# Four instead of two W_in blocks of the first pair in one-pass products, in a new instruction order

## The chip, the cores and the metric

The kernel runs on one core of one Trainium2 chip. The metric is the device time of one execution, in microseconds (us), as the median of the runs. The names of the engines in the profile are PE (matrix products), PEld (the loading of weights into PE), DVE, ACT, POOL and SP; SP only issues transfers here.

## What is computed

A chunked state-space scan over x, a, B and C (4 batches, 8 heads, 768 steps, head width 32, state width 16) gives 3072 rows of 256 numbers. These rows go through two matrix products with a silu between them.

```python
for c in range(nc):
    ...
    L = np.exp(cum[:, :, :, None] - cum[:, :, None, :]) * causal
    CB = np.einsum('bhin,bhjn->bhij', Cc, Bc)
    y_intra = np.einsum('bhij,bhjd->bhid', CB * L, xc)
    y_inter = np.einsum('bhin,bhnd->bhid', Cc, state) * decay_to_i[:, :, :, None]
    y[:, :, sl] = y_intra + y_inter
    state = decay_full[:, :, None, None] * state + np.sum(Bx, axis=2)
...
h = x @ w_in                          # (3072, 256) @ (256, 2048)
g = h * (1.0 / (1.0 + np.exp(-h)))
return g @ w_out                      # (3072, 2048) @ (2048, 256)
```

## The kernel before

The 3072 rows are worked on in 12 units of 256 rows; two units make a pair, so there are six pairs, 0 to 5. For each unit u the scan is a short chain over four engines: products of B and C (`g0`, line 585), products of x and B (`D` for units 0 and 1, `gd` later, line 571), a decay scan on DVE (`E`, line 512), the masking product on DVE (`M`, line 600, two halves), the running state on DVE (`S`, line 615) and its copy on ACT (`SM`, line 623), and at the end the unit's rows in PSUM (`Y`, lines 635 and 644).

W_in and W_out are each cut into 8 blocks, numbered 0 to 7 (W_in) and 8 to 15 (W_out). They arrive as 64-bit numbers, 512 KB a block (`lw`, line 288), and each is made into a 32-bit block by two ACT instructions (`u`, line 294, and `v`, line 297), three DVE instructions (`w,n,0`, `w,n,1`, `w,n,2`, lines 303, 307, 310) and an addition on POOL (`W`, line 318).

There are two ways to multiply by a block. In 32-bit form PE takes every product in two passes that the trace lists as two records; that is `s,u,j` (line 697: unit u, W_in block j) and `n1` (line 761: W_out for pair 0). In the other way both factors are split into three parts, named h, l and d: a rounded high part, the rest, and a correction. The product of the parts h and l (`a,G,i`, line 800) and of the parts d (`d,G,i`, the same line) goes for a whole pair at once in one pass for each part; `q` (line 782) is the same for W_out, with `qh` for the parts h and l and `qd` for d. `ax` and `dg` (lines 811 and 821, ACT) scale the sum between them and apply silu. The parts of a weight block come from `H` (ACT, line 322), `lD` (DVE, line 326) and `dD` (DVE, line 330), or for some W_out blocks from ACT copies and POOL transfers (`Wl`, `Wd`, `Wm`, `We`); the parts of a unit's rows come from `xh` (ACT, line 679) and `x,u,0` and `x,u,1` (DVE, lines 651 and 654, the l and the d part). For the silu outputs they are `h` (ACT, line 827), `l` (DVE, line 651) and `e` (DVE, line 837).

Pairs 1 to 5 use parts throughout. Pair 0 is done as the weights arrive: six of its eight W_in blocks in 32-bit form (`s`, each unit by itself, silu by `si`, line 703) and blocks 6 and 7 in parts (`a,0,6`, `a,0,7`); its W_out product is in 32-bit form (`n1`). For the 32-bit form a unit's rows are copied out of PSUM to one tile by `X0,u,0` and `X0,u,1` (ACT, line 666); `s` and `xh` read that tile. Products of even blocks are summed in the PSUM tile ga and those of odd blocks in gb, the two tiles that `g0`, `gd` and `Y` use too.

The order is written out by hand as a list of words, `SCHEDULE` (lines 18 to 100). Each word calls the function of that name and so appends its instructions to the in-order queues of the engines that it uses; no scheduler changes the order after that. `SLOTS` names the buffer that each tile takes in turn. The word `z,1` is a product of zeros that PE runs while it waits at the start (line 441). Loads with a queue number 0 go out by SP in the order of the list.

## Time and profile before

| what | us |
|---|---|
| median of three runs (329.33 to 329.74) | 329.33 |
| the profiled execution | 329.1 |
| its span, first to last instruction | 327.4 |
| PE busy in the span | 320.3 |
| DVE busy | 240.4 |
| ACT busy | 209.5 |
| POOL busy | 56.0 |

The profiled execution's own time is 1.7 us longer than its span, and 0.23 us shorter than the median. Times within the span are counted from its start. A matrix product's listed duration is its latency; consecutive products overlap, so what one costs on PE is seen from where a row of them starts and where the next one does. The same holds, to a smaller part, on DVE and ACT, where an instruction starts about 0.08 us before the one ahead of it is listed as ended.

### The profile page before, as it was taken

To read this page: it belongs to the slowest core of one execution; us is meant where nothing else is said; L and a number is where in the kernel's file an instruction comes from. 1 tells how busy PE (TensorE), PEld (TensorE's weight loads), DVE (VectorE), ACT (ScalarE), POOL (GpSimd) and SP (SyncE) were. 2 spreads that over 40 slices of the span, in tenths; PEclk is the share of its full clock that TensorE was granted. 3 is DMA by queue.
4 is the path that set the end of the run, shared out by engine and by line. 5 is a ranking of instruction groups with operands and counts; after the bars stand their busy time and mean duration, and the time that the engine had idled before them with its cause. 6 is when DMAs were issued, how large, how long until landed. Compare 5 with 4: busy or idle time off the path is not lost.

```text
span 327.4 us, 7519 instructions
## 1 busy us (share of the span) xinstructions
PE 320.3 (98%) x3064; PEld 243.4 (74%) x3067; DVE 240.4 (73%) x331; ACT 209.5 (64%) x319; POOL 56.0 (17%) x74
## 2 busy tenths in 40 slices
PE   8999999999999999999999999999999999999994
PEld 3478576655687777878887778878887788888883
DVE  4998999999988965877687299665787544635553
ACT  4679978648696846583771875837775455574641
POOL 1364766326102330001200010010001000000000
PEclk9999999999999999999999999999999999999999
DMA  6979966479872663423633306514042000050003
GB/s 162 206 200 272 296 175 192 51 148 135 148 127 46 105 115 53 86 36 64 147 74 70 44 1 117 104 26 96 3 74 37 7 2 2 0 88 0 2 1 64
DMA packets 94962, 29.27 MB, mean 89 GB/s; under 512 B 80000, under 2 KB 86912, under 8 KB 94928
## 3 DMA queue, kind: packets, MB, share of 16 engines
q1 hardware_dynamic: 90960, 25.71, 37.5%
q0 software_dynamic: 1616, 2.82, 5.1%
q10 hardware_dynamic: 2352, 0.26, 0.6%
q8 instruction: 24, 0.39, 0.5%
q14 instruction: 10, 0.08, 0.1%
HBM read 22.81 MB, written 3.34 MB: 80 GB/s over the span
## 4 chain that ended last, share of the span: by engine, by line
PE 94%; SPq 2%; DMA 1%; DVE 1%; issue 1%; DVEq 0%
PE hp L782 29%; PE ga L800 18%; PE gb L800 18%; PE hp L761 9%; PE hp L697 6%; PE o_ps L782 6%; PE ga L635 2%; PE ga L585 2%; PE ga L644 2%; DMA s2k<-in_C_dram 1%; PE gb L644 1%; PE ga L571 1%; SPq L262 0%; SPq L375 0%; PE o_ps L531 0%
## 5 line engine op out<-in xcount | busy, mean ns | idle before, releaser
L782 PE MATMUL hp<-r4k,s2k 128*128 128x512 f32 x400 | 110.0, 394 | 0.0
L651 DVE SCALAR_TENSOR_TENSOR r4k<-r4k,r4k 128x1024 fp32r<-128x1024 f32 (+1 forms) x42 | 50.5, 1202 | 51.3 <-ACT r4k L827 48.2
L782 PEld LDWEIGHTS hp<-r4k,s2k 128*128 128x128 f32 x400 | 74.0, 188 | 16.4 <-issue 0.3
L800 PE MATMUL ga<-raw,s2k 128*128 128x512 f32 x240 | 62.3, 395 | 0.0
L800 PE MATMUL gb<-raw,s2k 128*128 128x512 f32 x240 | 61.1, 390 | 0.0
L800 PEld LDWEIGHTS ga<-raw,s2k 128*128 128x128 f32 x240 | 44.7, 188 | 11.4 <-ACT ga L811 0.9
L800 PEld LDWEIGHTS gb<-raw,s2k 128*128 128x128 f32 x240 | 44.8, 188 | 9.9 <-ACT gb L811 0.5
L837 DVE SCALAR_TENSOR_TENSOR r4k<-r4k,r4k 128x1024 fp32r<-128x1024 f32 x40 | 49.2, 1231 | 3.4 <-DVE r4k L651 0.9
L827 ACT ACTIVATE r4k<-r4k 128x1024 fp32r<-128x1024 f32 x40 | 42.2, 1058 | 3.2 <-issue 1.3
L811 ACT ACTIVATE ga<-ga 128x1024 f32<-128x1024 f32 x21 | 21.1, 1007 | 24.6 <-PE ga L800 23.8
L811 ACT ACTIVATE gb<-gb 128x1024 f32<-128x1024 f32 x21 | 21.2, 1009 | 17.6 <-PE gb L800 13.3
L782 PE MATMUL o_ps<-r4k,s2k 128*128 128x512 f32 x80 | 30.7, 390 | 0.0
L761 PE MATMUL hp<-r4k,s2k 128*128 128x512 f32 x64 | 30.0, 602 | 0.0
L821 ACT ACTIVATE r4k<-gb 128x1024 f32<-128x1024 f32 x21 | 21.4, 1021 | 12.4 <-PE gb L800 9.9
L520 POOL TENSOR_TENSOR BT<-bn,ab 128x256 f32<-128x256 f32 x10 | 6.7, 672 | 129.5 <-DVE ab L512 123.3
L318 POOL TENSOR_TENSOR s2k<-s2k,s2k 128x512 uint32<-128x512 uint32 (+1 forms) x19 | 23.6, 1250 | 26.4 <-DVE s2k L307 13.7
L821 ACT ACTIVATE r4k<-ga 128x1024 f32<-128x1024 f32 x21 | 21.5, 1023 | 8.4 <-PE ga L800 8.2
L512 DVE TENSOR_TENSOR_SCAN ab<-ab,diag 128x512 f32<-128x512 f32 x20 | 24.8, 1265 | 0.0
L697 PE MATMUL hp<-r4k,s2k 128*128 128x256 f32 x96 | 22.3, 382 | 0.2 <-issue 0.2
L697 PEld LDWEIGHTS hp<-r4k,s2k 128*128 128x128 f32 x96 | 18.0, 190 | 4.0 <-issue 1.4
L761 PEld LDWEIGHTS hp<-r4k,s2k 128*128 128x128 f32 x64 | 11.6, 189 | 10.5 <-issue 9.6
L782 PEld LDWEIGHTS o_ps<-r4k,s2k 128*128 128x128 f32 x80 | 15.0, 188 | 3.2
(123 smaller groups left out, 384.8 us busy)
## 6 DMA issues: line engine op xcount, KB each, us to landing
ab<-az SPq DMA_DIRECT2D x20, 256.0 KB, 4.2
raw<-in_moe_w_in_dram SPq DMA_DIRECT2D x8, 512.0 KB, 4.2
raw<-in_moe_w_out_dram SPq DMA_DIRECT2D x8, 512.0 KB, 8.0
out_dram<-r4k SPq DMA_DIRECT2D x44, 64.0 KB, 2.0
xt<-in_x_dram SPq DMA_DIRECT2D x20, 128.0 KB, 4.2
s2k<-s2k POOLq DMA_DIRECT2D x10, 256.0 KB, 3.8
pfx<-ac SPq DMA_DIRECT2D x10, 130.0 KB
bn<-in_B_dram SPq DMA_DIRECT2D x20, 64.0 KB, 5.2
```

The lines of the kernel that those rows point to most:

```text
L318: nc.gpsimd.tensor_tensor(out=u[:, :, fs], in0=u[:, :, fs], in1=v[:, :, fs], op=ALU.add)
L512: nc.vector.tensor_tensor_scan(out=o, data0=src, data1=diag.rearrange("p h t -> p (h t)"), initial=0.0, op0=ALU.mult, op1=ALU.add)
L644: nc.tensor.matmul(out=y[w][32 * q:32 * q + 32, c, 64 * k:64 * k + 64], lhsT=xc[64 * c:64 * c + 64, k, h], rhs=m[64 * c:64 * c + 64, k, h] ...
L651: nc.vector.scalar_tensor_tensor(out=l, in0=f32(h), scalar=BACK, in1=y, op0=ALU.mult, op1=ALU.add)
L697: nc.tensor.matmul(out=hp[:, i], lhsT=WT[j][:, kc, 128 * i:128 * i + 128], rhs=XM()[:, 2 * kc:2 * kc + 2, u], start=(kc == 0), stop=(kc == ...
L761: nc.tensor.matmul(out=NP[m], lhsT=WT[8 + f // 2][:, f % 2, 128 * m:128 * m + 128], rhs=GT[0, f // 2][:, f % 2], start=(n == 1), stop=(n = ...
L782: nc.tensor.matmul(out=ACC[P, c], lhsT=WK[8 + i, p][:, k, 128 * m:128 * m + 128], rhs={"h": HT, "l": LT, "d": DT}[p][P, i][:, k], start=(n ...
L800: nc.tensor.matmul(out=o, lhsT=WK[j, q][:, kc, 128 * i:128 * i + 128], rhs=xs[:, 2 * kc:2 * kc + 2], start=(start and q == "h" and kc == 0 ...
L811: nc.scalar.activation(t, t, AF.Copy, scale=1.0 + Z)
L821: nc.scalar.activation(g, t, AF.Silu, scale=BACK)
L827: nc.scalar.activation(t, GT[G, i], AF.Copy, scale=-LESS * Z)
L837: nc.vector.scalar_tensor_tensor(out=DT[G, i], in0=f32(HT[G, i]), scalar=-1.0, in1=f32(LT[G, i]), op0=ALU.mult, op1=ALU.subtract)
```

## The change

Blocks 4 and 5 of W_in move, for pair 0, from the 32-bit form to parts. The words `s,0,4`, `s,1,4`, `s,0,5`, `s,1,5` and their four `si` go; `a,0,4`, `a,0,5`, `ax`, `d` and `dg` for the same two blocks come. No other word is added or removed: the other 1301 words are those of before, in another order, and so are the buffers that the tiles take. W_in blocks are loaded in the order 0, 5, 4, 2, 6, 1, 7, 3 instead of 0, 4, 7, 5, 1, 6, 2, 3. The first blocks that PE multiplies are 0 and 2 in 32-bit form and then 5 and 6 in parts; before they were 0, 4, 5 for unit 0, then 1, 5, 0, 4 and then 7 in parts. One of the 36 products of zeros ahead of the transpose `AT` moves behind it. All functions below line 102 are unchanged but for the buffer numbers in `SLOTS`.

The diff of the list at the start, at the first pair, around the start of pair 1's W_out products, and at the end:

```diff
 SCHEDULE = """
-Ln,0,0,0,1 ia,1 ci z,1 z,1 z,1 z,1 z,1 z,1 ia,0 Ln,0,0,1,1 cI z,1 ch cP ct ip,0,0 z,1 z,1 z,1 c1 cd A AT cp AU lw,0 z,1
+ci ch z,1 Ln,0,0,0,1 ia,1 z,1 Ln,0,0,1,1 ia,0 z,1 z,1 z,1 c1 cd cp cI co z,1 z,1 ip,0,0 A cP ct z,1 z,1 lw,0 AT AU
+as,1,1 as,0,0 tp,0 tq,0 P01,0,0 ab,0,0 z,1 z,1 z,1 z,1 Lx,0,0,0 as,0,1 P01,0,1 ab,0,1 Lt,0,1,3,0 E,0,0 B,0,0 u,0 w,0,0
 ...
-S,0,3 Ln,1,1,0,0 ab,1,0 E,1,0 C,0 Y,0 X0,0,1 Ln,1,0,1,0 B,1,1 X0,0,0 u,5 w,5,0 ip,1,0 z,1 P01,1,0 tp,1 tq,1 s,0,0 ce,1,1
-ce,1,0 g0,1 Lx,1,1,0 Lx,1,0,0 W,4 xh,0 w,5,1 si,0,0 B,1,0 P01,1,1 D,1 s,0,4 M,1,1 lw,1 u,1 lw,12 S,1,0 W,5 v,1 ca S,1,1
-S,1,2 SM,1,0 SM,1,1 lw,13 s,0,5 si,0,5 v,12 C,1 M,1,0 Y,1 w,1,0 w,1,1 W,7 si,0,4 lw,8 w,1,2 W,1,0 z,1 w,12,2 X0,1,0 H,7
-S,1,3 X0,1,1 x,0,0 lD,7 u,12 w,12,0 w,12,1 u,13 w,13,0 w,13,1 W,1,1 s,0,1 u,8 v,8 s,1,5 ir,3 w,8,0 si,0,1 s,1,0 co
-Ln,2,0,1,0 xh,1 W,12 x,1,0 w,8,1 v,13 w,13,2 W,13 lw,15 u,15 w,8,2 Ln,2,1,1,0 si,1,5 s,1,4 a,0,7 si,1,4 n1,9,0 H,12
-Wd,12 x,0,1 lw,14 u,14 n1,11,0 n1,9,1 x,1,1 W,8 Ln,2,1,0,0 v,14 w,14,2 ir,0 si,1,0 n1,1,0 n1,1,1 H,0 n1,0,1 H,1 lw,6 v,6
+z,1 z,1 z,1 M,0,1 ab,1,0 z,1 w,5,1 SM,0,1 lw,2 z,1 v,4 w,4,2 u,4 w,4,0 z,1 W,0,0 z,1 H,0 Ln,1,0,0,0 SM,0,0 C,0 z,1 w,5,2
+W,5 v,2 Y,0 w,4,1 u,2 Ln,1,0,1,0 E,1,0 Ln,1,1,0,0 X0,0,0 X0,0,1 xh,0 H,5 tp,1 tq,1 ce,1,0 w,2,2 ce,1,1 s,0,0 ip,1,0
+S,0,3 w,2,0 P01,1,0 w,2,1 P01,1,1 C,1 B,1,0 si,0,0 ca B,1,1 Lx,1,0,0 Lx,1,1,0 D,1 S,1,0 g0,1 S,1,1 S,1,2 SM,1,0 W,2,1
+W,2,0 s,0,2 M,1,0 W,4 lw,6 Ln,2,0,1,0 M,1,1 SM,1,1 Y,1 lD,5 v,6 w,6,2 u,6 w,6,0 X0,1,1 lw,1 x,0,0 X0,1,0 H,4 z,1 w,6,1
+x,0,1 s,1,0 W,6 ir,0 lw,10 lw,7 xh,1 S,1,3 u,1 w,1,0 H,6 x,1,1 x,1,0 w,1,1 v,1 w,1,2 W,1,1 Ln,2,1,1,0 s,1,2 u,10 lD,6
+lw,8 si,1,2 v,10 w,10,0 a,0,5 si,1,0 a,0,6 ax,0,6 w,10,1 si,0,2 ir,2 ir,1 w,10,2 u,7 W,1,0 s,0,1 u,8 W,10 v,8 ir,3 v,7
+s,1,1 dD,5 Ln,2,0,0,0 si,0,1 lw,3 v,3 n1,5,1 Ln,2,1,0,0 AA,0 Lt,3,1,0,0 dD,6 d,0,6 w,8,0 AD,4 H,10 Wl,10 n1,5,0 u,3
+dg,0,6 ax,0,5 w,8,2 w,7,0 n1,4,0 lD,4 tp,2 w,7,2 n1,4,1 lw,13 u,13 w,7,1 W,7 ce,2,0 H,7 w,8,1 W,8 w,3,0 a,0,4 n1,1,1
 ...
-u,2 W,6 n1,8,0 AD,1 v,2 H,6 v,10 w,2,0 s,1,1 si,1,1 lw,3 tp,2 dD,7 v,3 v,15 u,3 w,2,1 w,2,2 W,2,0 Lt,3,1,3,0 lD,6 dD,6
-w,14,0 n1,8,1 w,3,2 a,0,6 ax,0,6 w,15,2 W,2,1 s,1,2 si,1,2 H,2 d,0,7 w,14,1 dg,0,7 AD,2 w,3,0 w,15,1 d,0,6 dg,0,6 W,14
-Lt,3,1,0,0 w,10,2 s,0,2 lw,9 u,9 v,9 Lt,3,1,2,0 Lt,3,1,1,0 T,3,1 H,4 si,0,2 n1,10,0 Lx,2,0,0 n1,12,1 La,2,0,0 w,3,1 tq,2
-La,2,1,0 E,2,1 E,2,0 lD,4 w,9,0 W,15 n1,15,1 Lt,3,0,0,0 n1,12,0 B,2 ce,2,0 ce,2,1 Lt,3,0,3,0 g0,2 lw,11 u,11 Lp,2,0 C,2
-M,2,1 Lx,2,1,0 gd,2 b,2,0 b,2,1 S,2,0 S,2,1 H,15 S,2,2 W,3 Lp,3,0 Lt,4,1,1,0 H,13 La,3,1,0 w,10,0 v,11 Lt,4,1,0,0
-n1,15,0 SM,2,0 Wl,15 SM,2,1 w,10,1 W,10 ce,3,1 Lt,4,1,3,0 M,2,0 La,3,0,0 E,3,1 E,3,0 s,0,3 si,0,3 Lt,3,0,2,0 ce,3,0
+n1,0,1 w,3,1 AA,1 d,0,5 lw,15 v,15 w,13,0 AP AD,0 v,13 si,1,1 ce,2,1 dg,0,5 lw,14 w,13,1 lD,7 w,13,2 W,13 n1,0,0 w,3,2
+W,3 n1,1,0 n1,10,0 Lt,3,1,3,0 a,0,7 s,0,3 u,15 H,13 w,15,0 v,14 w,14,2 u,14 w,15,1 w,15,2 W,15 lw,12 u,12 dD,4 ax,0,4
+dD,7 d,0,4 tq,2 n1,11,1 lw,9 u,9 ax,0,7 w,12,0 n1,11,0 AD,1 w,14,0 v,9 w,9,2 v,12 w,12,2 d,0,7 La,2,0,0 w,12,1 La,2,1,0
+E,2,0 E,2,1 Lt,3,0,2,0 Lt,3,1,1,0 H,15 Lx,2,0,0 w,9,0 si,0,3 w,9,1 B,2 Lt,3,0,1,0 Lp,2,0 C,2 dg,0,7 s,1,3 Lx,2,1,0
+La,3,1,0 dg,0,4 n1,10,1 Wd,13 si,1,3 g0,2 M,2,1 gd,2 b,2,0 S,2,0 W,12 Lt,3,0,0,0 b,2,1 S,2,1 n1,15,0 w,14,1 S,2,2
 ...
-SM,4,1 n1,14,0 n1,6,0 SM,4,0 Lt,5,1,3,0 M,4,0 n1,7,0 Vn,0 Y,4 y,4,1 y,4,0 xh,4 l,1,0 n1,7,1 S,4,3 a,1,2 Vn,1 lD,9 dD,8
-dD,2 H,5 a,1,1 ax,1,2 e,1,0 q,1,0,1,0 d,1,2 dD,9 q,1,0,0,1 Ln,5,0,0,0 ax,1,1 d,1,1 Wd,13 Lt,5,1,1,0 q,1,0,0,0 q,1,0,1,1
-AD,3 Lt,5,1,0,0 dD,4 dg,1,2 Lt,5,0,3,0 h,1,2 a,1,4 dg,1,1 h,1,1 Lt,5,1,2,0 T,5,1 ce,5,0 Lt,5,0,2,0 ce,5,1 Lt,5,0,0,0
+Lt,4,0,0,0 T,4,0 La,5,0,0 g0,4 lD,1 dD,1 n1,6,0 Lp,4,0 Ln,5,0,0,0 M,4,1 b,4,0 b,4,1 S,4,0 S,4,1 H,9 S,4,2 Wl,13 M,4,0
+SM,4,0 C,4 Lx,5,1,0 SM,4,1 Wl,12 n1,12,0 lD,8 n1,7,0 Vn,0 Ln,5,0,1,0 Y,4 y,4,0 lD,2 dD,2 H,3 dD,8 lD,3 Lt,5,0,3,0 y,4,1
+xh,4 Wm,12 n1,7,1 a,1,2 a,1,1 We,12 o,0,0,2 La,5,1,0 dD,10 ax,1,2 l,1,0 e,1,0 d,1,2 x,4,1 Lx,6,0,0 Lt,5,0,2,0 Vn,1
+o,0,1,2 Wm,13 ax,1,1 O,0,0,2,2,0 x,4,0 E,5,1 q,1,0,1,1 dg,1,2 h,1,2 l,1,2 q,1,0,0,1 E,5,0 H,11 Wl,11 La,6,1,0 Wm,15
 ...
-h,5,6 l,5,6 q,5,5,0,0 q,5,4,1,1 q,5,5,1,0 qh,5,6,1,1 e,5,6 q,5,6,0,0 dg,5,7 h,5,7 q,5,6,1,0 l,5,7 q,5,4,1,0 qh,5,7,1,1
-e,5,7 q,5,7,0,0 q,5,7,1,0 qd,5,7,1,1 Va,5,0 Vd,5,0 o,5,0,2 O,5,0,2,0,0 O,5,0,2,3,0 qh,5,6,0,1 qh,5,7,0,1 q,5,4,0,1
-Va,5,1 qd,5,6,0,1 qd,5,6,1,1 qd,5,7,0,1 Vt,5,1,1 O,5,0,2,2,0 Vt,5,1,0 ot,5,1,0 or,5,1,0 O,5,0,2,1,0 os,5,1,0,0 Vt,5,1,2
-Vt,5,1,3 ot,5,1,1 or,5,1,1 os,5,1,1,1
+qh,5,6,0,1 e,5,7 qh,5,7,1,1 qh,5,7,0,1 q,5,7,1,0 q,5,7,0,0 Va,5,0 Vd,5,0 o,5,0,2 O,5,0,2,2,0 O,5,0,2,0,0 q,5,5,1,1
+O,5,0,2,1,0 qh,5,6,1,1 q,5,4,1,1 qd,5,7,1,1 qd,5,7,0,1 O,5,0,2,3,0 qd,5,6,0,1 Va,5,1 Vt,5,1,0 Vt,5,1,1 ot,5,1,0 or,5,1,0
+os,5,1,0,0 Vt,5,1,3 Vt,5,1,2 ot,5,1,1 or,5,1,1 os,5,1,1,1
 """
...
 SLOTS = {
...
```

## The prediction

> **What bounds the kernel now.** I read the page first: the busy shares, the two rows of slices, the chain.

> ```profile
> span 327.4 us, 7519 instructions
> PE 320.3 (98%) x3064; PEld 243.4 (74%) x3067; DVE 240.4 (73%) x331; ACT 209.5 (64%) x319; POOL 56.0 (17%) x74
> PE   8999999999999999999999999999999999999994
> DVE  4998999999988965877687299665787544635553
> PE 94%; SPq 2%; DMA 1%; DVE 1%; issue 1%; DVEq 0%
> ```

> PE is full but for the first and the last slice, and the chain is PE for 94%. Work taken from PE is therefore worth its full length, unless PE then waits. The second thing to see is the DVE row: nearly full until about 100 us, loose after that. Stretches show how tight it is:

> ```profile
> 16.00:26.00 10.00, 9.70 (x272) 7.58 (x265) 8.84 (x19) 6.98 (x16) 6.10 (x8) 1.00 0.82 223
> 26.00:56.00 30.00, 29.84 (x138) 20.95 (x123) 28.94 (x40) 26.26 (x48) 17.69 (x20) 1.00 0.82 227
> 56.00:90.00 34.00, 34.00 (x546) 20.53 (x545) 32.29 (x52) 22.19 (x47) 12.24 (x14) 1.00 0.73 124
> ```

> The columns are the length, then PE, PEld, DVE, ACT and POOL busy, the granted clock, the DMA share and GB/s. From 26 to 90 us DVE rests 1.06 + 1.71 = 2.8 us in 64 us, and PE does not wait. How PE comes to be full is in the timeline of its start:

> ```profile
> 17.94 1.99 PE L697 MATMUL hp<-r4k,s2k 128*128 128x256 f32 x8
> ...
> 21.07 3.77 PE L697 MATMUL hp<-r4k,s2k 128*128 128x256 f32 x16
> 24.77 0.27 PE L635 MATMUL ga<-cw,sm 32*64 32x64 f32 x2
> ...
> 26.41 7.07 PE L697 MATMUL hp<-r4k,s2k 128*128 128x256 f32 x32 [0.16 <-issue]
> ```

> `s,0,0` starts at 17.94, `s,0,4` and `s,0,5` at 21.07, unit 1's `Y` at 24.77, and four more `s` follow at 26.41. From 17.94 on PE is never short of work; what is ahead of it is a scan chain filled with products of zeros.

> **The change part by part.** *PE work.* The chain gives throughput without the latency:

> ```profile
> 43.04 1.73 PE hp L697 x8
> ...
> 88.51 1.82 PE gb L800 x8
> ...
> 100.08 0.91 PE gb L800 x4
> ```

> One `s` (8 records) is 1.73 us; one `a` (8) is 1.82, one `d` (4) is 0.91. Four `s` go, 6.92 us; two `a` and two `d` come, 5.46. PE has 1.46 us less to do: **-1.46**.

> *Up to `s,0,0`: 0.* The words ahead of it are the same kinds. One product of zeros fewer stands before the transpose `AT`, and the C tiles of unit 0 are asked for ahead of the second W_in block, both for the good of the scan; against that `SM,0,0` now stands behind `v,4`, `u,4` and `H,0` on ACT, so that unit 0's `Y` waits for the third load. I leave 17.94 as it is; bounds -0.4 (one of the first ten products of zeros, 4.45 / 10 = 0.44) and +0.6 (one ACT `u` of 0.69, shown below, less 0.08 of overlap).

> ```profile
> 1.27 4.45 PE L441 MATMUL o_ps<-s2k 128*128 128x512 bf16 x10 [1.27 <-DVE s2k L388]
> ...
> 13.84 1.04 PE L441 MATMUL o_ps<-s2k 128*128 128x512 bf16 x4
> ```

> *Between `s,0,0` and unit 1's `Y`: 0.* Before, three `s` run here, now two. With everything else alike `Y` would start at 24.77 - 1.73 = 23.04, one `s` less being done: no gain, no loss. What may hold it back is unit 1's masked product, the last thing that `Y` needs from DVE:

> ```profile
> 22.98 0.68 DVE L600 TENSOR_TENSOR ab<-ga,ab 128x512 f32<-128x512 f32 x1
> ```

> It ended at 23.66, 1.1 us before `Y` started. The DVE instructions ahead of it are the same set in both orders (four blocks' `w`, four scans, seven states), so it comes at 23.66 or, with the 0.4 above, a little earlier. I take 23.04; bounds 0 (PE has nothing to run sooner) and +0.6 (23.66).

> *Behind unit 1's `Y`: +0.45.* Before, `s,0,1` stood between `Y` and `s,1,5`, the first product that needs unit 1's rows, and the copies `X0` ran under it.

> ```profile
> 26.50 0.37 ACT L666 ACTIVATE r4k<-ga 128x256 f32<-128x256 f32 x1
> 26.76 0.62 ACT L322 ACTIVATE s2k<-s2k 128x512 fp32r<-128x512 f32 x1
> 27.28 0.38 ACT L666 ACTIVATE r4k<-gb 128x256 f32<-128x256 f32 x1
> ```

> Now the next product behind `Y` is `s,1,0`, with one product of zeros between. The cover is gone: PE waits for both copies, 0.26 (start to start) + 0.38, with some 0.05 to start, 0.7 us. The product of zeros fills 0.26 of it (1.04 / 4), but one stood there before too, on top of the work, so the loss is 0.7 - 0.26, or 0.45 rounded; bounds 0.4 and 1.2, the latter if `v,6` or `u,6`, ahead of the copies on ACT, is still waiting for its load, as an ACT `u` did before:

> ```profile
> 22.10 0.69 ACT L294 ACTIVATE s2k<-raw 128x512 f32<-128x512 f32 x1 [1.52 <-DMA raw<-in_moe_w_in_dram]
> ```

> That was the fifth load; `lw,6` is the fifth now, behind the same bytes, so it lands near 22.1, 2 us before the copies.

> *`a,0,5` two products later: +0.1.* It needs `x,1,0` on DVE, the tenth instruction after the mask: `lD,5`, `w,6` (2), `x,0,0`, `w,6`, `x,0,1`, `S`, `w,1`, `x,1,1`, `x,1,0`. From rows

> ```profile
> 24.51 0.69 DVE L310 SCALAR_TENSOR_TENSOR s2k<-raw,s2k 128x512 uint32<-128x512 uint32 x1
> ...
> 27.17 0.27 DVE L615 SCALAR_TENSOR_TENSOR st<-st,s2k,hp 128x64 f32<-128x64 f32 x1
> 27.36 0.68 DVE L651 SCALAR_TENSOR_TENSOR r4k<-r4k,r4k 128x512 fp32r<-128x512 f32 x1
> 27.96 0.68 DVE L326 TENSOR_TENSOR s2k<-s2k,s2k 128x512 fp32r<-128x512 f32 x1
> 28.57 0.41 DVE L303 TENSOR_SCALAR s2k<-s2k 128x512 f32<-128x512 f32 x1
> ...
> 33.60 3.47 DVE L654 SCALAR_TENSOR_TENSOR r4k<-r4k,r4k 128x512 fp32r<-128x512 f32 x2
> ```

> that is six of 0.68, three of 0.41 and one of 0.27, less 0.08 of overlap each: 4.8 us from about 22.9, and with the wait for `xh,1` and `u,1` on ACT some 28.5 to 29. PE is through with `s,1,0` and `s,1,2` at 23.04 + 1.5 (`Y`) + 0.7 + 3.46 = 28.7. It is a near thing: 0 to 1.1 us, the latter if one `x` takes 1.73 us, as each of the two L654 did, and not 0.68. What stood beside those two is POOL's addition:

> ```profile
> 33.15 3.37 POOL L318 TENSOR_TENSOR s2k<-s2k,s2k 128x512 uint32<-128x512 uint32 x2 [2.24 <-DVE s2k L310]
> ```

> I take 0.1: only one addition (`W,6`) falls into this stretch, and the wait for ACT covers it in part.

> [...]

> *DVE up to 90 us: +0.1.* DVE's total is unchanged, but by the first d part of pair 1 (`e,1,0`, which `q,1,0` needs) it must also have done `lD,5`, `dD,5`, `dD,4`, `dD,10`, `lD,3` and `o,0,0`, and no longer `lD,9` and `S,4,3`:

> ```profile
> 86.82 1.22 DVE L837 SCALAR_TENSOR_TENSOR r4k<-r4k,r4k 128x1024 fp32r<-128x1024 f32 x1
> ...
> 90.17 0.84 PE L782 MATMUL hp<-r4k,s2k 128*128 128x512 f32 x3
> ```

> Six of about 0.6 less 0.6 and 0.2 is +2.8 us. The room is DVE's rest, 2.8 us, and the 90.17 - 88.04 = 2.1 us that the part was early: 4.9 us. It fits. 0.1 stands for a short wait; bounds 0 and +4.4 (all six doubled, below).

> *The rest: 0.* From 100 us on DVE is loose (slices mostly of 5 to 8 tenths) and every pair has the same words as before. At the end four d products run while ACT copies the sum of the others,

> ```profile
> 321.30 0.92 PE o_ps L782 x4
> ```

> and the new list ends with four such products too (the d of `q,5,4,1,1` and three `qd`); what follows is alike. Bounds ±0.2, one product.

> The sum: -1.46 + 0 + 0 + 0.45 + 0.1 + 0.1 = **-0.8**. Against the profiled execution's 329.1 that is 328.3; the median of the runs stands 0.23 higher, so **328.5** against 329.33.

> **The rivals.** *DVE falls behind (slower).* Decided in the stretch from 26 to 90 us. If four of the six instructions moved ahead fall on POOL additions, each takes 1.1 us more (1.73 - 0.68, rounded up): 2.8 + 4.4 = 7.2 against 4.9 of room, 2.3 us of waiting ahead of `q,1,0` or a `Y`. -0.8 + 2.3 = +1.5, 330.8. It decides from two such collisions on (2.8 + 2.2 = 5.0). For it: DVE is busy 28.94 of 30 us. Against: the number of additions is the same, so what is hit here is spared elsewhere. [...]

> *The start gives it all back (no change).* `Y` of unit 1 at 23.66 (+0.6) and `x,1,0` hit by `W,6` (+0.2 instead of 0.1): -0.1, 329.2. For it: three near things follow each other on PE with no other product between. Against: the mask was 1.1 us early before.

> *The start gains.* `s,0,0` 0.4 earlier and the masks with it, nothing lost at `a,0,5` or at 90 us: -1.46 - 0.4 + 0.45 = -1.4, 327.9. For it: C's tiles stand behind one W_in block fewer. Against: the ACT order ahead of unit 0's `Y`.

> **How the numbers follow.** The forecast (328.5, its own range 328.1 to 328.9) has 0.42, the start that gains 0.13, no change 0.19, DVE behind 0.22; 0.04 is left for a wait after 100 us. A measurement of this kernel can tell about 0.2% from no change, 0.66 us: 328.67 to 329.99 is "same". Faster: 0.13, and 0.39 of the forecast and its neighbours, 0.52. Same: 0.20, most of the second rival. Slower: 0.28, DVE behind, the rest of no change, and what is left. Range 327.7 to 330.5: the lower end is the start that gains with the end's 0.2, the upper takes in the greater part of DVE behind.

> **What would show it.** Right: L697 with 64 records instead of 96 and L800 with 24 more; unit 1's `Y` starting near 23.0; behind it a hole of 0.4 to 0.5 us on PE ahead of L697; `a,0,5` starting within 0.2 us of the end of `s,1,2`; no PE idle around 90 us; DVE's rest from 26 to 90 us under 2 us. Wrong: a wait of L800 or L782 for DVE's L651, L837 or L330 of over 0.5 us, a wait of `Y` for L600, or means of `lD` and `dD` well above these:

> ```profile
> L330 DVE SCALAR_TENSOR_TENSOR s2k<-s2k,s2k 128x512 fp32r<-128x512 f32 x12 | 8.4, 715 | 0.1
> ...
> L326 DVE TENSOR_TENSOR s2k<-s2k,s2k 128x512 fp32r<-128x512 f32 x10 | 7.5, 756 | 0.0
> ```

## The result, and the profile after

The changed kernel takes 334.41 us (median of five runs, 333.69 to 335.43) against 329.33 for the kernel before; the ratio is 1.0151, with a 95% interval from 1.0123 to 1.0178. It is 5.1 us slower, where 0.8 us faster was forecast.

The five runs spread by 1.7 us, and their mean granted clock with them (last section); the profiled execution is the fastest. The page of the changed kernel looks almost like that of the kernel before, and this execution took 333.69:

```profile
span 332.0 us, 7491 instructions
...
PE 319.7 (96%) x3059; PEld 241.7 (73%) x3059; DVE 236.0 (71%) x331; ACT 211.8 (64%) x319; POOL 57.6 (17%) x74
...
PE   8897999999999999999999998999999999999993
...
PE 84%; DMA 4%; SPq 3%; DVE 3%; ACT 2%; issue 1%; POOL 1%; DVEq 0%; ACTq 0%
```

The span is 4.6 us longer and PE is busy 0.6 us less: PE has less to do and waits more. Of the 40 slices, each 8.3 us, the second and the fourth lost most (8 and 7 where 9 stood), and one at 200 us lost something (8). The list of what each PE group waited for names the places:

```profile
PE gb L644 <- issue: 1.8, 1, 1.8
PE ga L585 <- DVE bh L525: 1.4, 1, 1.4
...
PE ga L635 <- issue: 0.9, 1, 0.9
PE hp L697 <- POOL s2k L318: 0.6, 1, 0.6
...
PE hp L697 <- ACT r4k L666: 0.4, 1, 0.4
```

The columns are the total, how often, and the longest. The kernel before has none of the first three. The 0.9 us of L635 stand ahead of unit 0's `Y`, which starts right behind ACT's `SM,0,0` (below). The largest is new in kind: `Y` (L644) waited 1.8 us for "issue", that is for nothing that the profile shows, once, in its midst. The timeline of PE around it:

```profile
18.22 1.91 PE L697 MATMUL hp<-r4k,s2k 128*128 128x256 f32 x8
...
21.87 1.99 PE L697 MATMUL hp<-r4k,s2k 128*128 128x256 f32 x8 [0.58 <-POOL s2k L318]
23.80 0.27 PE L635 MATMUL ga<-cw,sm 32*64 32x64 f32 x2
...
24.42 0.34 PE L644 MATMUL ga<-ab,s2k 64*32 64x64 f32 x16
24.56 0.29 PE L644 MATMUL gb<-ab,s2k 64*32 64x64 f32 x8
26.66 0.26 PE L644 MATMUL gb<-ab,s2k 64*32 64x64 f32 x4 [1.81 <-issue]
...
28.06 3.72 PE L697 MATMUL hp<-r4k,s2k 128*128 128x256 f32 x16 [0.42 <-ACT r4k L666]
31.43 2.19 PE L800 MATMUL gb<-r4k,s2k 128*128 128x512 f32 x8
```

After 24 of unit 1's 64 such products PE stops, though the rest of `Y` needs the same two tiles as its start. Then it goes on as if nothing had been. What was missing is in part 3 of the page, which lists a queue of transfers that no line of the kernel issues:

```profile
q8 instruction: 24, 0.39, 0.5%
q14 instruction: 11, 0.08, 0.1%
```

q8 brings 24 packets of 16 KB (0.39 MB). PE has 6182 records in the trace (products, weight loads and semaphore waits), or 258 to a packet. Counted in the trace, PE stops at its 705th record. In a later run (e8) it stops at its 449th, 256 records away, so a packet is taken here as the code of 256 PE records; the counts are good to a record or two. The views of the transfers in the stretches 20.0 to 24.2 us (first) and 24.0 to 26.0 us (second) show when that code came:

```profile
DMA packets 1664, 1.09 MB, mean 260 GB/s; under 512 B 1174, under 2 KB 1174, under 8 KB 1664
...
q1 hardware_dynamic: 1664, 1.09, 93.3%
```

```profile
DMA packets 453, 0.75 MB, mean 373 GB/s; under 512 B 100, under 2 KB 100, under 8 KB 452
...
q1 hardware_dynamic: 452, 0.73, 100.5%
q8 instruction: 1, 0.02, 3.1%
```

In the first stretch there are only the kernel's own loads, and they fill 93% of the DMA engines; the one code packet comes in the second, from 24.25 to 25.23, and PE goes on 1.4 us behind its end. In the kernel before the same packet came 3 us sooner, 21.25 to 23.15, with PE at its 705th record only at 25.51. This table is counted from the traces (PE records in order of start, and the second packet of q8):

```
                 449th record   packet         705th record
before           19.88          21.25-23.15    25.51, no stop
after            20.07          24.25-25.23    24.63, the next at 26.66
```

The other two losses. At 200 us the products of unit 9 wait for DVE, and DVE for a load, the quarter of B that SP issued at 195.98, behind a group of stores (L719). The list puts DVE's wait down to the load of x issued later, but DVE transposes B here, and e3 moves this one load:

```profile
192.73 2.58 SPq L719 DMA_DIRECT2D out_dram<-r4k  x4
...
195.98 0.59 SPq L262 DMA_DIRECT2D tbc<-in_B_dram  x1
...
199.91 0.64 DVE L525 STREAM_TRANSPOSE bh<-tbc 128x256 f32<-128x256 f32 x1 [1.99 <-DMA xt<-in_x_dram]
...
200.69 0.32 PE L585 MATMUL ga<-ce,bh 32*64 32x128 f32 x2 [1.44 <-DVE bh L525]
```

At the end the time from the last products of W_out (L782) to the last instruction has grown from 327.4 - 321.14 = 6.26 to 332.0 - 324.71 = 7.29. The last products, and then the transfers from 328.6 to 330.1 us, in 40 slices and by queue:

```profile
324.71 1.07 PE L782 MATMUL o_ps<-r4k,s2k 128*128 128x512 f32 x4
```

```profile
DMA  9999999899899795516000000000001101010000
...
q10 hardware_dynamic: 272, 0.13, 32.0%
q1 hardware_dynamic: 107, 0.05, 11.0%
q14 instruction: 1, 0.01, 1.5%
```

The last store (q10, 272 packets) is through at 329.3 but for 9 packets. Those come one by one up to 330.0, behind a packet of 8 KB on the second code queue, q14, that took from 329.30 to 329.66.

Where the 4.6 us of span went: the first product behind unit 1's `Y` starts at 28.06 instead of 26.41 (1.65) and has 0.27 more product work behind it (six `s`, four `a` and four `d`, against nine, two and two); 1.44 at 200 us; 1.03 at the end. That is 4.4; 0.2 is spread.

### The profile page after: what moved, and what is told of

Same layout as the page of the kernel before. It is cut to its first block, busy times and chain, and to the rows that moved or that the text cites. A ratio compares the mean times of both kernels' runs of the same rounds, so it can differ in the third digit from the quotient of the medians.

```text
span 332.0 us, 7491 instructions
## 1 busy us (share of the span) xinstructions
PE 319.7 (96%) x3059; PEld 241.7 (73%) x3059; DVE 236.0 (71%) x331; ACT 211.8 (64%) x319; POOL 57.6 (17%) x74
## 4 chain that ended last, share of the span: by engine, by line
PE 84%; DMA 4%; SPq 3%; DVE 3%; ACT 2%; issue 1%; POOL 1%; DVEq 0%; ACTq 0%
PE hp L782 26%; PE ga L800 17%; PE gb L800 17%; PE hp L761 7%; PE o_ps L782 5%; PE hp L697 4%; DMA raw<-in_moe_w_in_dram 2%; PE ga L635 1%; PE ga L585 1%; PE ga L644 1%; SPq L262 1%; PE gb L644 1%; PE ga L571 1%; DMA pfx<-ac 1%; SPq L719 1%
## 5 line engine op out<-in xcount | busy, mean ns | idle before, releaser
L782 PE MATMUL hp<-r4k,s2k 128*128 128x512 f32 x400 | 109.7, 393 | 0.0
L782 PEld LDWEIGHTS hp<-r4k,s2k 128*128 128x128 f32 x400 | 74.0, 188 | 16.3 <-issue 0.5
L651 DVE SCALAR_TENSOR_TENSOR r4k<-r4k,r4k 128x1024 fp32r<-128x1024 f32 (+1 forms) x42 | 50.0, 1193 | 41.0 <-ACT r4k L827 39.3
L800 PE MATMUL ga<-raw,s2k 128*128 128x512 f32 x240 | 62.4, 395 | 0.0
L800 PE MATMUL gb<-raw,s2k 128*128 128x512 f32 x240 | 61.2, 390 | 0.0
L800 PEld LDWEIGHTS ga<-raw,s2k 128*128 128x128 f32 x240 | 44.8, 188 | 11.2 <-issue 1.0
L837 DVE SCALAR_TENSOR_TENSOR r4k<-r4k,r4k 128x1024 fp32r<-128x1024 f32 x40 | 49.0, 1226 | 4.9 <-PE o_ps L782 2.1
L800 PEld LDWEIGHTS gb<-raw,s2k 128*128 128x128 f32 x240 | 44.7, 188 | 10.1 <-ACT gb L811 0.5
L811 ACT ACTIVATE ga<-ga 128x1024 f32<-128x1024 f32 x22 | 22.2, 1010 | 27.4 <-PE ga L800 23.7
L520 POOL TENSOR_TENSOR BT<-bn,ab 128x256 f32<-128x256 f32 x10 | 8.3, 826 | 140.7 <-DMA bn<-in_B_dram 93.2
L811 ACT ACTIVATE gb<-gb 128x1024 f32<-128x1024 f32 x22 | 22.2, 1009 | 15.8 <-PE gb L800 15.8
L821 ACT ACTIVATE r4k<-gb 128x1024 f32<-128x1024 f32 x22 | 22.5, 1024 | 13.8 <-PE gb L800 13.7
L821 ACT ACTIVATE r4k<-ga 128x1024 f32<-128x1024 f32 x22 | 22.5, 1024 | 13.3 <-PE ga L800 8.1
L782 PE MATMUL o_ps<-r4k,s2k 128*128 128x512 f32 x80 | 30.7, 390 | 0.0
L318 POOL TENSOR_TENSOR s2k<-s2k,s2k 128x512 uint32<-128x512 uint32 (+1 forms) x19 | 24.5, 1302 | 25.4 <-DVE s2k L310 16.5
L512 DVE TENSOR_TENSOR_SCAN ab<-ab,diag 128x512 f32<-128x512 f32 x20 | 25.3, 1282 | 0.9 <-DMA ab<-az 0.9
L600 DVE TENSOR_TENSOR ab<-gb,ab 128x512 f32<-128x512 f32 x12 | 8.3, 690 | 17.4 <-PE gb L585 17.4
L761 PEld LDWEIGHTS hp<-r4k,s2k 128*128 128x128 f32 x64 | 11.5, 189 | 9.6 <-issue 7.8
L782 PEld LDWEIGHTS o_ps<-r4k,s2k 128*128 128x128 f32 x80 | 15.0, 188 | 3.2
L697 PE MATMUL hp<-r4k,s2k 128*128 128x256 f32 x64 | 15.0, 382 | 1.0 <-POOL s2k L318 0.6
```

Source lines behind the costliest of these rows:

```text
L318: nc.gpsimd.tensor_tensor(out=u[:, :, fs], in0=u[:, :, fs], in1=v[:, :, fs], op=ALU.add)
L512: nc.vector.tensor_tensor_scan(out=o, data0=src, data1=diag.rearrange("p h t -> p (h t)"), initial=0.0, op0=ALU.mult, op1=ALU.add)
L520: nc.gpsimd.tensor_tensor(out=BT[u][:, ks], in0=bn[u][:, ks], in1=E[u][:, ks, :, Q - 1:Q].to_broadcast([128, n, H, N]), op=ALU.mult)
L651: nc.vector.scalar_tensor_tensor(out=l, in0=f32(h), scalar=BACK, in1=y, op0=ALU.mult, op1=ALU.add)
L697: nc.tensor.matmul(out=hp[:, i], lhsT=WT[j][:, kc, 128 * i:128 * i + 128], rhs=XM()[:, 2 * kc:2 * kc + 2, u], start=(kc == 0), stop=(kc == ...
L761: nc.tensor.matmul(out=NP[m], lhsT=WT[8 + f // 2][:, f % 2, 128 * m:128 * m + 128], rhs=GT[0, f // 2][:, f % 2], start=(n == 1), stop=(n = ...
```

## The experiments

**e1 and e2: is the stop in `Y` the code's or the data's?** Both leave the words as they are and change only how many records stand ahead of `Y`. e1 adds five products of zeros, each two records:

```diff
-... W,5 v,2 Y,0
+... W,5 v,2 z,1 z,1 z,1 z,1 z,1 Y,0
```

> The changed kernel with five more products of zeros (ten PE records) just ahead of unit 0's Y, where PE waits anyway. In the changed kernel PE stood still for 2.0 us inside unit 1's Y, ahead of its 705th record, while a 16 KB packet of PE's code arrived from 24.25 to 25.23 us. Theory 'code': PE had run out of code, and the end of a block of code is at a fixed record number. Then the gap stays at the 705th record from the start (705 +-2), which is now ten records earlier in Y, and begins after a fetch that starts at 22 us or later; its length may be anything from 0.5 to 3 us. Rival 'data': an operand of that product came late; then the gap stays at the same product of Y, record 715, whatever the count. Time within 1 us of the changed kernel by both.

One run, 335.10. The stop is again at the 705th record:

```profile
24.02 0.34 PE L644 MATMUL ga<-ab,s2k 64*32 64x64 f32 x16
24.15 0.27 PE L644 MATMUL gb<-ab,s2k 64*32 64x64 f32 x3
26.72 0.28 PE L644 MATMUL gb<-ab,s2k 64*32 64x64 f32 x7 [2.30 <-issue]
```

19 products instead of 24 were done: five products, or ten records, less for ten records more ahead. No product of `Y` waits for its data there; PE stops at a place in its code. In e2 the last twenty products of zeros ahead of unit 0's `Y` become four small ones each (64 x 64), 120 records more, so that the 705th record lies ahead of unit 1's `Y`:

```diff
-z,1
+z,0,4
```

> The changed kernel with the last 20 products of zeros ahead of unit 0's Y made of four small ones each (64x64 in place of 128x512): 120 more PE records in the same waits. Theory 'code': the block ends 120 records earlier in the work, ahead of unit 1's Y, and the request for the next block is made some 3 us earlier (inside unit 0's Y), so that it is there in time: no gap over 0.5 us inside unit 1's Y, and 1.5 to 2.5 us less than the changed kernel (about 332). Rival 'data': the gap inside unit 1's Y stays at 2 us and the time at 334. Rival 'it moves': the gap is as long but elsewhere, time 334.

331.9 (six runs), ratio 1.0076 (1.0049 to 1.0103), 2.5 us faster than the changed kernel, whose interval lies clear above. `Y` runs without a stop, and the products behind it start 2.4 us sooner:

```profile
25.71 3.72 PE L697 MATMUL hp<-r4k,s2k 128*128 128x256 f32 x16 [0.43 <-ACT r4k L666]
29.08 2.19 PE L800 MATMUL gb<-r4k,s2k 128*128 128x512 f32 x8
```

**e8: the same in the kernel before.** Its last twenty products of zeros made small.

> The kernel before with the last twenty products of zeros ahead of unit 0's Y made small, as was done to the changed kernel. Theory (small products helped the changed kernel only because its PE stopped for code in Y, which the kernel before does not): within 0.3 us of the kernel before. Rival (small products are better by themselves, since unit 0's Y starts sooner): 0.5 to 2.5 us faster than the kernel before, as in the changed kernel.

330.71 (eight runs, 329.32 to 331.98), ratio 1.0039 (1.0018 to 1.0061): slower, where the theory had no change and the rival a gain. The trace, of the slowest run, shows a stop:

```profile
16.24 0.28 PE L644 MATMUL gb<-ab,s2k 64*32 64x64 f32 x4
18.27 0.28 PE L644 MATMUL gb<-ab,s2k 64*32 64x64 f32 x6 [1.75 <-issue]
```

Unit 0's `Y` now holds PE's 449th record, 256 ahead of the 705th, and stops there. (This execution also ran for 3.4 us at half the clock behind the stop, and the two fastest runs, 329.32 and 329.57, are hardly slower than the kernel before, 329.30 on that chip; how long the stop was in them no trace shows.) The edit that removes the stop from one kernel makes one in the other: it is the place of the 256-record blocks in the work that counts, not the small products.

**e4: why the code came late.** Four of the loads of weights behind unit 1's `Y` are issued by ACT in its own order instead of by SP, the first of them behind the copy `X0,1,0`.

```diff
-lw,1 ... lw,10 lw,7 ... lw,8
+lw,1,1 ... lw,10,1 lw,7,1 ... lw,8,1
```

> The changed kernel with four weight loads (blocks 1, 10, 7 and 8) issued by ACT behind unit 1's copies and not by SP as soon as it can, so that the transfer engines have little to do between 20 and 27 us. Theory 'the code waits behind the loads': the second fetch of PE's code starts by 22.5 us instead of 24.25, and the gap inside unit 1's Y is under 0.7 us. Rival: the fetch starts when PE gets near the end of its block, whatever the traffic; then it starts at 24 us or later and the gap stays near 2 us. The time itself says little: block 1 comes later, and a,0,5 with it by 1 to 4 us.

The first fence has two rows of the stretches (the last two columns are the DMA share and GB/s), the second one of the timeline. The DMA engines are full up to 22 us and 36% busy from 22 to 24 us, and the packet comes at 22.27 to 23.41, 1.9 us behind PE's 449th record instead of 4.2. `Y` doesn't stop, and the products behind it start at 26.25:

```profile
20.00:22.00 2.00, 1.64 (x66) 0.95 (x64) 1.73 (x6) 1.17 (x3) 1.73 (x3) 1.00 0.99 206
22.00:24.00 2.00, 1.95 (x12) 1.46 (x12) 2.00 (x5) 1.72 (x4) 1.23 (x1) 1.00 0.36 58
```

```profile
26.25 3.72 PE L697 MATMUL hp<-r4k,s2k 128*128 128x256 f32 x16 [0.43 <-ACT r4k L666]
```

As a repair it is worthless (338.66, one run): the weights come later for it, and from 30 us on PE waits 4.7 us behind DVE. But with these loads moved the packet came sooner and the stop was gone. In the five traces that have the change's loads as they were and their 449th record between 19 and 21 us (the changed kernel, e1, e3, e6, e12), the packet comes 3.3 to 5.3 us behind that record. How full the DMA engines are does not decide it by itself: in the kernel before, e2, e5, e7, e9, e10 and e11 it came 1.4 to 2.2 us behind the record, with a DMA share of 0.9 or more up to then. So the loads bear on when the packet comes; which of them it waits for stays open.

**e3: the load at 200 us.** One word is moved ahead of the stores.

```diff
-y,8,0 Lt,9,0,2,0 y,8,1
+y,8,0 Lt,9,0,2,0 Lt,9,0,1,0 y,8,1
```

> The changed kernel with one load (a quarter of B of unit 9, the fourth of its kind) asked for ahead of eleven stores of results on SP's queue and not behind them. Theory: the 1.7 us that PE stood still ahead of unit 9's g0 near 200 us was this load, issued only after the stores; then that gap is gone and the time is 1.3 to 1.7 us less than the changed kernel (about 332.9). Rival: another operand of g0 (the copies of C, or the buffer in PSUM) comes as late; then under 0.5 us is won.

333.52 (four runs, 333.10 to 335.42), ratio 1.0120 (1.0081 to 1.0160), 0.9 us less than the changed kernel; the two intervals overlap, so in the times the gain isn't shown. In the trace it is: unit 9's products (L585) follow at 200.02 on the W_out products with no wait. That execution ran for 3.4 us at half the clock (last section), and a pair of `s` in it took 5.41 us instead of 3.72; by that some 1.7 us were lost, more than the 1.44 gained; its stop in `Y` was shorter, 0.9 us.

**e6: the end.** 16 instructions of DVE that set a column of an unused tile to zero, near 250 us, where DVE is loose.

```diff
+    "k": lambda n: [nc.vector.memset(pad[:, 0:1], 0.0) for _ in range(n)]
-... a,4,4 ax,4,4
+... a,4,4 k,16 ax,4,4
```

> The changed kernel with 16 tiny DVE instructions (a column of an unused tile set to zero) near 250 us, nothing else. Theory A (the 8 KB code packet that lands at 329.3 in the midst of the last store is DVE's, asked for at its 448th record or so): the packet comes some 10 us earlier, the last store takes 0.6 instead of 1.3 us, and the tail from the last product to the end shrinks from 7.3 by 0.7 to 1.0 us. Theory B (it is another engine's, or the tail is long for another reason): the packet and the tail stay where they are. The stop in Y stays at 2.0 us and the stop at 200 us at 1.4 by both.

333.12 (one run). The last q14 packet comes at 314.9 instead of 329.3 (315.2 in the kernel before), and the last store is not held up; the transfers from 329.0 to 330.1 us, in 40 slices:

```profile
DMA  9999999999999999999997431000000000000000
```

The store takes 0.62 us instead of 1.31, and from the last turn of the rows (L739) to the end it is 331.4 - 326.65 = 4.75 us instead of 332.0 - 326.23 = 5.77. So the packet was DVE's code, and 16 more instructions brought it forward. The changed kernel has 15 DVE records fewer than the kernel before (450 and 465), and with them the packet came later, in the midst of the last store.

**e7 and e5: the wait for W,2.** DVE does block 2's two steps ahead of unit 1's `S` and `P01`; e7 with the small products, e5 with the load, the 16 DVE instructions and the small products.

```diff
-S,0,3 w,2,0 P01,1,0 w,2,1
+w,2,0 w,2,1 S,0,3 P01,1,0
```

> The changed kernel with the last twenty products of zeros ahead of unit 0's Y made small, and w,2,0 and w,2,1 ahead of S,0,3 and P01,1,0 on DVE. Theory: W,2 runs 0.4 to 0.6 us earlier on POOL, s,0,2 starts at about 21.1 instead of 21.55 with no wait for POOL, unit 1's Y starts at the later of 23.0 and the end of the mask, which comes up to 0.4 later than 22.94 since two DVE steps of 0.4 now stand ahead of P01; s,1,0 near 25.3 instead of 25.7. Rival: the mask takes the place of the wait, Y stays at 23.5 and nothing is gained.

> The changed kernel with four repairs at once: the last twenty products of zeros ahead of unit 0's Y made small (more PE records ahead of Y), the late load of unit 9 put ahead of the stores, W,2's two DVE steps put ahead of unit 1's P01 so that s,0,2 doesn't wait for POOL, and 16 tiny DVE instructions near 250 us that leave everything else alone but move DVE's own place in its code. Theory (the change is worth its 1.46 us of PE work, and what hides it is the PE stop for code in Y, 2.5 us; the load at 200 us, 1.3; the wait for W,2, 0.5; and the tail, 1.0): 333.7 - 5.3 = 328.4, that is 0.9 to 1.2 below the kernel before. Rival (the one-pass products are not worth anything at this place, the start of the DVE chain loses what they save): not below 329.6 even with all repairs, with new waits of PE for DVE between 26 and 100 us.

e7: 333.01 (one run), and the wait has moved, as its rival had it, only further. `s,0,2` doesn't wait for POOL; unit 1's `Y` waits for `SM`, and the products behind it start at 27.02, 1.3 us later than in e2:

```profile
20.09 1.46 POOL L318 TENSOR_TENSOR s2k<-s2k,s2k 128x256 uint32<-128x256 uint32 x2 [0.36 <-DVE s2k L307]
20.12 0.84 DVE L475 TENSOR_SCALAR s2k<-s2k 128x256 f32<-128x256 f32 x1
```

`P01` (L475) now runs beside POOL's additions for W,2 and takes 0.84 us, where it took 0.49 in e2, and its scan (L479) 1.10 instead of 0.68; all of unit 1's chain is behind them, and its mask ends at 24.75 (22.94 in e2). e5, with this order in it, comes to 330.17 (twelve runs, 329.47 to 330.57), ratio 1.0018 (1.0004 to 1.0032): near its rival, and the move is dropped.

**e9 to e12: what the change is worth without the stops.** e9 is e5 with block 2's steps where the change had them. e10 also puts `SM,0,0` ahead of `H,0` on ACT, which unit 0's `Y` had waited behind. e11 is e10 with other small products, the tenth to the twenty-fifth product of zeros instead of the last twenty; e12 is e11 with the small ones added to those products and not in their place.

```diff
-H,0 Ln,1,0,0,0 SM,0,0 C,0
+SM,0,0 H,0 Ln,1,0,0,0 C,0
```

> The changed kernel with three repairs: the last twenty products of zeros ahead of unit 0's Y made small, unit 9's late load put ahead of the stores, 16 tiny DVE instructions near 250 us. W,2's DVE steps are where the change had them. Theory (each loss is by itself: the stop in Y 2.5, the load about 1.3, the tail 1.0): 333.7 - 4.8 = 328.9, 0.4 below the kernel before (329.3), and 0.8 to 1.3 below the version with W,2's steps moved as well, which lost that much ahead of unit 1's Y. Rival (the stops take each other's place, as the wait for the mask took W,2's): 329.8 or more, no better than 330.2.

> The same, with SM,0,0 put ahead of H,0 on ACT, so that unit 0's Y doesn't stand behind the 0.6 us of H,0. Theory: Y of unit 0 at about 15.5 instead of 16.05, and s,0,0, s,0,2 and s,1,0 earlier by 0.3 to 0.5: 328.5, the time that was predicted for the change itself. Rival (code or W,2 is late then, so that PE only waits in another place): s,0,2 or unit 0's Y stops for W,2 or at PE's 449th record, s,1,0 comes at 25.7 as without it, no difference to the other version by more than 0.2.

> The same with four small products added to each of those sixteen, which keep their own: 128 more records and PE never shorter of work than the changed kernel. Theory: as the other, and the clock never falls to a half; the added products cost up to 0.1 us each where the scan doesn't cover them, 328.4 to 329.2. Rival: the added products push the first transposes back and everything behind them, 330 or more.

```
       us (runs, lowest to highest)     before, same chip   ratio, 95%
e9     330.10 (12, 328.83 to 330.74)    329.46              1.0006 (0.9986 to 1.0026)
e10    329.55 (12, 328.46 to 330.51)    329.46              0.9999 (0.9982 to 1.0015)
e11    329.54 (12, 328.60 to 330.20)    329.50              0.9989 (0.9968 to 1.0009)
e12    334.45 (6, 332.87 to 335.03)     329.50              1.0134 (1.0104 to 1.0164)
```

e9, e10 and e11 can't be told from the kernel before. The stops in unit 1's `Y`, at 200 us and in the last store are gone from all three; with them went 4.3 (e9) to 4.9 us (e11) of the 5.1, by medians that were not taken side by side (334.41 - 330.10 and 334.41 - 329.54); part of it is not the stops', since the small products alone start unit 0's `Y` 0.4 us sooner (16.06 in e2, 16.43 in the changed kernel). No version beats the kernel before beyond its interval. What PE still waited for in e10 and in e11:

```profile
PE hp L571 <- DMA s2k<-in_x_dram: 0.8, 1, 0.8
PE gb L644 <- issue: 0.5, 1, 0.5
...
PE hp L697 <- ACT r4k L666: 0.4, 1, 0.4
```

```profile
PE hp L697 <- POOL s2k L318: 0.8, 1, 0.8
PE hp L697 <- ACT r4k L666: 0.7, 1, 0.7
```

So the rivals were right in part: x of unit 1, block 2 and the copies `X0` hold PE by turns once the code doesn't. In e10 a smaller stop (0.48) stands at the 449th record, in e11 one of 0.25. e12 missed: its added products pushed unit 0's `Y` back by some 4 us, and PE stopped at its 705th record again, for 2.3 us (packet 25.19 to 26.23).

## Why the prediction was wrong, point by point

*PE work, -1.46.* As counted: L697 has 64 records instead of 96, L800 has 48 on tiles r4k instead of 24, and two `s` still take about 3.4 us (28.06 to 31.43). No run shows the saving by itself, but e10, which has none of the three losses, shows where it goes. From the first `s` behind unit 1's `Y` to the last four W_out products it takes 321.07 - 25.98 = 295.09 us, the kernel before 321.14 - 26.41 = 294.73: 0.36 longer, for 0.27 more work. Behind `Y` the balance is as counted. Ahead of it there is one `s` less, 1.73 us, and the `s` behind `Y` starts only 0.43 us sooner; the rest goes into the waits above.

*Up to `s,0,0`, 0.* 18.22 instead of 17.94, within the bounds. The reason was the one named: `SM,0,0` behind `v,4`, `u,4` and `H,0`, of which `v,4` waited for its load:

```profile
14.30 0.68 ACT L297 ACTIVATE s2k<-raw 128x512 f32<-128x512 uint32 x1 [0.56 <-DMA raw<-in_moe_w_in_dram]
...
15.97 0.37 ACT L623 ACTIVATE sm<-st,par 128x96 f32<-128x96 f32 x1
```

*Between `s,0,0` and unit 1's `Y`, 0: the step that failed.* It asked what `Y` needs and found the mask, with at most 0.6 to lose. The mask was early, as argued (23.26, before 23.66):

```profile
22.58 0.68 DVE L600 TENSOR_TENSOR ab<-gb,ab 128x512 f32<-128x512 f32 x1
```

Two things were left out. The smaller is block 2, `s,0,2`'s own factor, whose addition waited on POOL for DVE: 0.58, so that `Y` started at 23.80, not 23.04 and outside its bound of 23.66. The larger is that `Y` also needs its instructions. The stop for them cost 1.8 us, and that it is the code's is shown by e1 (same record, ten records sooner in the words), e2 (moved off `Y`, gone) and e8 (made in the kernel before).

Two things make it up, by the table above. Before, `s,0,4` and `s,0,5`, 3.5 us with few records, stood between the 449th record and `Y`. One of them went, and the time from the 449th to the 705th record shrank from 5.63 to 4.56 us. The prediction costed this `s` as work on PE alone; it was also cover under which the next block of code came in. And the packet itself came 4.18 us behind the 449th record, not 1.37. An estimate from these figures, with PE going on 1.43 us behind the packet's end as it did: with the late packet and the cover of before PE would still have stopped for 1.0 us; with the packet as early as before, 3.27 us from the 449th record to its end, and the short cover, for 0.1. So the late packet weighs more than the lost cover. e4 ties it to the loads, whose order the change altered too; the exact reason stays open. The q8 row stands on the page of before, and its trace has the packet at 21.25; the prediction used neither.

The coming of the code was not hidden under the work: PE stood for 1.8 us here and for 1.75 in e8.

*Behind unit 1's `Y`, +0.45.* Right: 0.42, and 0.43 in e2, 0.75 in e11.

*`a,0,5`, +0.1.* No wait, here or in e2 (29.08, 3.4 us behind the first `s`).

*DVE up to 90 us, +0.1.* Right in that PE waited for no DVE there. In the changed kernel itself the stop gave DVE time; in e2, without a stop, PE has no such wait either. The budget behind it was off: DVE's rest from 26 to 90 us was to fall from 2.8 us to under 2, and it was 9.5 in the changed kernel and 7.9 in e10, where PE doesn't stop there. Why DVE had so much more rest no run shows. Nor does one show the bound of +4.4, six steps each doubled: from 26 to 90 us the changed kernel's PE waited for "issue" (1.8 us) and ACT (0.4) alone; in the whole span its twelve `dD` took 10.9 us instead of 8.4, its ten `lD` 7.1 instead of 7.5, and the two L654 on tiles r4k 1.4 instead of 3.5. So the rival "DVE falls behind" had the sign and not the mechanism; that its sign came true was luck.

*The rest, 0 (bounds 0.2).* Failed twice. "Every pair has the same words as before" was true of the kinds and not of their order on SP's queue: the load behind the stores cost 1.44. "What follows is alike" was true of the words and not of DVE's code: with 15 records fewer a packet of it came under the last store, 1.03 with the wait behind it (e6).

## What to carry to other kernels

When an edit removes long products that have few instructions, ask what arrived while they ran; here the code of the short products behind them was part of it (the packet from 21.25 to 23.15 us in the kernel before). Read the instruction queue of the profile, see when its packets come in the old order and in the new, count the records to the next block (256 from one stop to the other here), and see whether a burst of short products stands on it right behind a stretch full of loads. An unexplained wait for "issue" in the midst of a group whose data was there was the sign here (1.8 us in `Y`); at the start of a group it can be a wait for data, as the 0.9 us ahead of unit 0's `Y` were. In a new order compare each queue's order too, SP's above all, down to the last store.

## What the runs showed of the hardware

PE stopped for 0.48 to 2.3 us at its 449th or its 705th record in eight traces (1.81 in the changed kernel, 2.30 in e1, 0.90 in e3, 1.75 in e8, 0.48 in e10 and 2.26 in e12 among them), with a packet of its code just landed, and went on 1.2 to 1.6 us behind the packet's end. The packet for the 705th came between 1.4 us (before) and 5.7 us (e8, which stood still for 2.0 of them) behind PE's 449th record. In e4 it came sooner with four loads moved; what asks for it, and when, the traces don't show.

The granted clock fell to 0.50 for a while in some executions, behind a pause of PE. The stretches of e9, the last columns being clock, DMA share and GB/s:

```profile
16.00:18.00 2.00, 1.61 (x88) 1.43 (x88) 2.00 (x5) 1.47 (x5) 1.31 (x1) 0.70 0.89 148
18.00:20.00 2.00, 2.00 (x16) 1.75 (x8) 2.00 (x7) 1.97 (x6) 1.40 (x4) 0.50 1.09 232
20.00:22.00 2.00, 2.00 (x51) 1.42 (x56) 1.12 (x4) 1.28 (x4) 1.90 (x3) 0.94 1.02 251
```

What the three rows lack to a clock of 1, times their 2 us, over one half, (0.30 + 0.50 + 0.06) x 2 / 0.5, is 3.4 us at half the clock; it was the same in e1, e3 and e8, and 6.8 us in e4. `s,0,0` took 2.51 us in it instead of 1.91, and the pair of `s` in e3 5.41 instead of 3.72. PE had paused for 1.8 us in e9 and e8, 0.9 and 0.4 in e3, 2.3 in e1 and 4.7 in e4. But after a pause of 1.8 us in the profiled execution of the changed kernel, 2.1 in e7 and 2.3 in e12 the clock stayed at 1.00. The runs of two kernels part by it: the changed kernel took 333.69 and 333.77 with a mean clock of 0.997 and 335.19 and 335.43 with 0.992, e9 328.83 to 329.51 with 0.996 or more and 330.00 to 330.74 with 0.995 or less. Those of e11 don't: 328.60 with 0.998, 330.20 with 1.000.

The length of the pause does not part the two (0.9 to 4.7 us ahead of the half clock, 1.8 to 2.3 us with the clock left at 1.00); what decides it no run shows. By an estimate from e3's rows (5.41 - 3.72), where the clock fell behind a pause of PE, that cost some 1.7 us on top of the pause.
